# Block-sparse attention with a gated convolution network: one written-out instruction order replaced by another

## The chip, the cores and the metric

The kernel runs on one core of one Trainium2 chip. The metric is device time in microseconds (us). Three runs of the kernel before took 207.28 us in the median (207.2 to 207.51). One further execution was taken by the hardware profiler; every row of a profile below is from such an execution.

## The reference

Inputs are q, k, v of 4 batches, 8 heads, 768 tokens and 64 dims, a table of sampled blocks, and three weights (512x1024, 3x1024, 1024x512). Cut to what is computed:

```
scores = q @ k.T / sqrt(64)
mask   = band of 32-token blocks | first/last block row and column | 3 sampled key blocks per query block
attn   = softmax(where(mask, scores, -1e9));  x = heads joined of (attn @ v)     # 768 x 512 per batch
h      = relu(x @ w_in)                                                          # 768 x 1024
conv   = 3-tap convolution of h along the tokens, one weight per channel
out    = (h * sigmoid(conv)) @ w_out                                             # 768 x 512
```

## The kernel before, in words

**Pairs, segments, units.** Heads are taken in pairs; pair P = 4b + j holds heads 2j and 2j+1 of batch b, 16 pairs in all. The query tokens of a batch are cut in two segments of 384 tokens; the last of the eight is cut again into 256 and 128, so segments are numbered 0 to 8. Within a segment the program goes through its four pairs, their two heads and six key chunks, in blocks of 128 keys by 128 queries. Eight blocks are a **unit**; units are numbered 0 to 143 and are in the same order in both kernels.

**One unit.** TensorE writes the scores of a unit into one of two PSUM tiles `st` of 1024 columns (L762; the mask is 24 extra rows of both operands, with -8000 where a key block is left out). ScalarE takes the exponential of the tile into one of six tiles `pt` (L774). TensorE multiplies `pt` with the values (L799) into one of two PSUM tiles `av`, 65 columns a block, the 65th being the sum of the weights. Unit 0 is split in two halves with a tile `st` each. After the last unit of a pair, VectorE takes the reciprocal of the sums (L707) and multiplies (L709) into `xtok`.

**From attention to the network.** `xtok` is transposed into `xT`, for segments 1 to 6 by a DMA transpose that SyncE issues (L718), for segments 0, 7 and 8 by TensorE and a copy (L728). When the four pairs of a segment are there, TensorE multiplies `w_in` with `xT`, eight groups of 128 channels (L896, tile `mix`), ScalarE (L916) or VectorE (L918) takes the relu, VectorE computes the convolution (L954 multiplies, L962 adds), ScalarE the tanh that stands for the sigmoid (L1001), VectorE the gate (L1004, L1009 into `gT`). For segment 8 TensorE does the convolution (L973, L978). The `w_out` product takes 128 tokens at a time (L831), ScalarE (L327) or VectorE (L331) copies it out to `o2s`, and SyncE sends it (L840).

**Loads.** Batch 0 and half of batch 1 come in untransposed; TensorE transposes q and k (L460, L500, L522), and copies put them into the tiles `t`. Later pairs go through DMA transposes into `stg`. Most loads are issued by GpSimd (L239); tiny copies into `pace` (L407, L673) hold GpSimd back until a unit's exponential or an earlier load is there. 45 products of zeros (L230) stand at the start to keep TensorE running.

**What sets the order.** The program first makes a list of 1787 steps, each a small function that emits one or a few instructions. `put_down` reads the string `ORDER`: two characters name a step, one letter the engine where a step may go to two of them (P, A, V for TensorE, ScalarE, VectorE), one character the buffer for each tile that the step takes. The steps are emitted in just that sequence, so the order on each engine, the choice between ScalarE and VectorE and the buffer numbers all come from the string. Engines work in their own order; semaphores hold a step until its inputs are there and its buffer is free. A step that waits holds all steps behind it on its engine.

Of the kernel before, what the change touches and what calls it, by code (L numbers as in the profile page):

```python
# [25 lines left out]
6y36g2016h6B16C6D46l1RV1QV2wV36m16G06H6u1s1n6v6z5Y06I51p4X1w4Y2X14Z1x4+2Z14/2+501y511z5234222V5ZV21V6n26P16Q6R0
6A6E6F6U06V6J6K1j6o6L06M6p06W16S06Z16+6T6N16qV6OV1r6/2720732e02fV2gV743ih16X77178iiik07f07g794il1q7k17l7h51i
ijV002KV47m0in16Y707p07q7r1imViF0iGiHiI71ioipV17u17v7w2iJiq0ir7C075762z1isViK2AV42BV7D7H17I7E32C07a7b17i7j7niN1
7c17J42s17M07N2tV7o7s7t7x537R17S2DV2uV2EViO147y7O57z2iP7AiQiz1iLiR7T03007W07X7Y17diAit082183iBA2842iu870887F17G
ivV37K7L2N18938c18d7PiM07Q7U7V2OV02PViw07e1iS312/18h0ixiyV8i7Z7+0852Q17/0iV2iW8e48j58p18q3823j38r0868a8b8f8u08v  # L30
2SViT80iYiX8w18g8k8l8z18A2RV7BiC08s18B28E08FiD8G3iU8J18K8L4iEVj918R08S8tja8x8T58y8C8D8W18H8X8I36254378/090iZi+
j13jf0jg8Y09112YV0j28m18nj4j333V32Vi/941958M8N08U8V8Z8+92939c09d962j5j01mj63919h19ijh979e498jbj7j89j5ji158O29m0
9n9r19sjc818ojjA09o1jdA13ajo0jp9w09t29909a35V18P3f3g33cV3bV553i3d0562F057jl1jmjnA9x9E19FjqV3eV2jJ08Q23k09y3ju0
jv9f09g9J0jKjM9K9G0jLjwVjN9k9l9p3h3o2T13p19q9L49O19Pjr19u2G09T09U9v9z2HV2IV9Q5jO9B19Cjs9/1jx09A19V2jyjzAa0a139D
9b3r3s0jtVjR1jSjP3w1jUjA1jBa402U0jCA3l9Ha5a91aaa619I9M9NjD1jEae09Raf9Sab42VV2WVaj1jFAjZ2jTjVjQj+ag53u3tjWak9W9X
jG0a20jH9Y2k09Zj/al0jIAar0a3a7a8kv13Dacasadaw1axjXjYkj0ahat3ay1aB0aiamaCan1auavkk3E13G3Ak1k53k6k7k8k9k29+k3k4
aD4kaaG1aHao1azaAkwaI5aO0aEaFaPklkx3B23F3M3N0aQ2aT1aUaV0kbkckmknV23nVapaJkyaY0aZb11b2aK3v43xkzA33qV33zV3yVa+3
b31kE0kFkB1kCb60b7aR0aS3H0aL0be1kDV14kGAkZ0k+k/l0kK0kLbfaWb84kMAbg5kH1kIbj0kJV53I1bkkQ0l1bl2kRkSAbo1kT13P3Q23S
kAjekobpaXbt0a/bub0b4l2bq03mVaMl51l6bv3kN0kOb5kUl8kPV6ld2bB1bCb9ba1bb2bD1kVA7kW0bG0bHbhkXbI4bibmbnbL1brl73R3XbM
bcbsbwbxbQ0bRaq03T0jkaNkYAbN5bS2kd1bd3JbE0bFkebV1bWkp0lelfl9lall3c10l3lg3CV4lhkqbJbKkrl41by1lbbObPbX0c2c61lic33  # L40
3UkfkgkhA3bzlmljlolnlplcc7c813OV0bAkslqlk3LVbTbUlz1bYcb0ccbZ1c4cg1lrls3KV3VV13WVcd4ktA1b+0b/c5c9cachci5lAlBcelC
lDA2co0cpct1cfculI0lF1lGlHVlJlKVm10cjm2m4cq0cv3cy0czm3m5cD1ckcEcA4cF53+3/343403Y141kilt1lL0cr0cl2cmcI0lMlNAcscJ
lulO0lPcwcQ1cK2cR4c4d0m6lQVm91mam7mbmcm8cS1lvlwcxcV0cWcBcCcG3ZV1c+1c/cHlxA0cX3d04lR0cL42494hd30d4c01441cN1mdcO
d50lSlU1cM1lTAlVdb1dccTcUmelWVmh2mimfdg0lX0dhl+1mklYl/dd5lZVdl1cYcZdi2d1dmd2d6d7de0m0Adn1cnmjmgku4i0dq0drd80mp3
d9mrmlmqmsmx0ds3lE4e4fdv1mtdwmD1dfdx4mmmElycP45dD0dEdI1djdkdF5dodpdtdJdudymydN0dadz1dGdHdOmnmudK24q4r1dP1dA2mo
mFmzdBmvmwdS1dT46V247VdU3mAmBV34a24gd+0d/mGdLe31dMdQe4mHV1e04e52dC24jmY0e80mV1e9mWdRed1dVeemZdW4v4n4s4tea04E4F2
mXV08m+VdX1nh0njdY4w1ei0n21n3ejm/0n0ef5e10eq1ere2e6e7ebdZmI4o0ek14Jn1A94bV2ev0n50ecewes4ninkn4Anlegehex2np1el
em1eA1eBeC0en0nq4kV3eonsepn6etn7Aaeun81n9eF0eGeN1eOnaAnx2eyezeDnb0nceH5eS0eEeTeInrnt4lVeP1eJne1eX1eYeQ0eK2eL4u
4m4xnyndAbeU4eZ2nmnunznfnAmJ0mKeRngVnF3nGnB4pV3f00eVeMmLf1f51eWf6nvnnnHno0f25mP1mQmMfd0fef71mNA2ff4nCnInwnJ4yV4
mRe+e/fi1mSfjf34zVnDmTA0fn0f4o30o4fk2o5Ao61foo7fs1ftfp54G4Bo8Vot0ounEov4C14H4I4PnKnL4Q2fu3nN0nOf8f91fa1nMnT1ow  # L50
fA0fBnUfgnPfF1nVmC4K0484LoxfbfC04DA4fGfH1oyfhnQnRV1fK0nWflfLnZ0fmnXV3n+fc04RV0oz4MV04NVo01o1fP1fM4fQfU0fqfrfvfV
fwn/Ao2AfR2oAol1omfx0onfW5oofyopfD0oc0g01g1g23o91fEodg50oeAg6g70oqfInSoafJobVoB2oDoCof0ga1fNgbfOgc1fSoggf0ggoi1
fTfXfY1ojg3g4g8orohAgh4okAgn1gog9gs0gtoEfZ2osoX0oYgdmOnYfzf+oFoJ3oLgp2oKoMoGmU4A4Ogx1geoHgu5gygigjgq0oR1oSgrgv
gwf/gG0gHgk1oNoIgz3gloOgL1gMgI0gN1gAoToZgBoPoQoUo+gQ0gC0oVV1gDgRgZ1p71g+gS4g/2p8p9pah20h3h71o/V2h45pbV3gmpd0pe
pg1phpfV1cpiVh8hg0pm0pnh93poApB0pDpj1pkhhhl1gE0plAdgJ1gKgOgPhmgFA1hi0oWp0hn1pp1ps0gTgUpqh00h1h5pCpEhq0h6ptpFpG
prAehahbhrpuApJ1pKhs4gV2gWpLpMhz1hj1hc1pNhdhAgX1gYVpHpR2hkpOpv0pwhohe1hE0hFhphthuhfApxAfpy1pzpI1pSp10p2hB2hG5
pAAhv0pThwpPhC0hN1hOhP3p3hDhx1pUpQpVpWhyVhW0hHhJ2p4p5A0qk1hI1qlpZ3hKp+p/qmAghXqq0qrh/1hY0qsAhq0pXq1qB0qDq2qR1pY
q3qChQqh1hRq4qihL0i0i80i9hMA2hZ0h+q50q6i11i2q7q8qjAiia4i41hS0i5qn1i30ibqt2hTicquqSq9A1qwid2qEi60qoi7AqpAjqb0qc
ieqFhU1hVAqvqGqdif1qJ3igAqxpcqHqeqfA2ri1rjrkAqyqKqIqLqMqzr90rarbArA1qUqArf1rBrC0qNrgrhArc0rl0rmrdrn2qgqap6reAqO
qTrorprDqPqVqQrv1rwr31rq0r4rrrs2rtrurx3qWryrzrErL0rR1rF0r5rMrGrHrNrOqXqYrIrSrTrUr6rJA3rPA2rKrVVrWrQr7A1r8qZ0q+  # L60
# [997 lines left out]
```

## Time and profile before

| | before |
|---|---|
| median of three runs | 207.28 us |
| the profiled execution, first to last instruction (span) | 205.4 us |
| median less that span (the profiled execution has no other time of its own) | 1.9 us |
| TensorE products, busy | 197.1 us (96%) |
| TensorE weight loads, busy | 142.3 us (69%) |
| ScalarE, busy | 189.7 us (92%) |
| VectorE, busy | 184.9 us (90%) |
| GpSimd, busy | 59.4 us (29%) |

How to read it: busy is the union of the instructions' durations on an engine. TensorE's products overlap in its pipeline, so their busy time holds latency too, and their mean duration is longer than the distance from one to the next. ScalarE's and VectorE's durations also overlap a little with the next instruction's. The three engines are all busy for nine tenths of the span, so no single share tells which one sets the end at a given place.

### The profile page before, as it was taken

The page shows a single profiled execution, that of the slowest core. Times are in us where ns is not written, and L with a number is a line of the kernel's source. Part 1 is how long each engine was busy: PE and PEld are TensorE (multiplying, and loading weights), DVE is VectorE, ACT ScalarE, POOL GpSimd, SP SyncE. Part 2 cuts the span into 40 slices and gives each one's busy share as a digit, 9 for nine tenths or more (in the row PEclk, how much of TensorE's full clock was granted, in tenths as well). Part 3 has the DMA queues.
Part 4 walks back from the last instruction along what each step waited for, and adds up shares of the span by engine and source line. Part 5 has one row for each costly group of instructions (what it writes and reads, how often), then busy time and mean ns, then how long its engine had stood idle before and what let it go on. Part 6 is the DMA issues. An engine that isn't in the chain of part 4 may idle for free.

```text
span 205.4 us, 6237 instructions
## 1 busy us (share of the span) xinstructions
PE 197.1 (96%) x2392; PEld 142.3 (69%) x2409; DVE 184.9 (90%) x572; ACT 189.7 (92%) x253; POOL 59.4 (29%) x113
## 2 busy tenths in 40 slices
...
GB/s 155 196 190 154 186 178 114 197 127 88 154 150 126 125 103 138 218 166 163 95 105 226 97 117 123 175 154 126 14 174 88 21 123 51 3 2 3 153 3 204
DMA packets 50969, 25.59 MB, mean 125 GB/s; under 512 B 36764, under 2 KB 47996, under 8 KB 50940
## 3 DMA queue, kind: packets, MB, share of 16 engines
...
q10 hardware_dynamic: 288, 0.30, 0.5%
q14 instruction: 10, 0.08, 0.1%
HBM read 23.09 MB, written 6.29 MB: 143 GB/s over the span
## 4 chain that ended last, share of the span: by engine, by line
PE 68%; ACT 15%; DVE 12%; issue 3%; ACTq 0%; DVEq 0%
PE st L762 22%; PE mix L896 15%; PE mix L831 15%; PE av L799 12%; ACT pt L774 11%; DVE m L954 3%; DVE t L331 2%; DVE m L962 2%; ACT m L1001 1%; DVE xtok L709 1%; PE st L831 1%; ACT vt L327 1%; DVE diag L379 1%; ACT hE L916 1%; PE mix L728 1%
## 5 line engine op out<-in xcount | busy, mean ns | idle before, releaser
L774 ACT ACTIVATE pt<-st 128x1024 bf16<-128x1024 f32 (+1 forms) x145 | 142.2, 1051 | 4.2 <-PE st L762 3.7
L762 PE MATMUL st<-t 88*128 88x256 bf16 (+2 forms) x600 | 90.5, 267 | 2.3 <-DVE t L331 1.2
L799 PEld LDWEIGHTS <-pt 128*128 128x128 bf16 x1152 | 54.0, 97 | 14.2
L762 PEld LDWEIGHTS <-t 88*128 88x128 bf16 x600 | 48.9, 97 | 21.0 <-issue 1.9
L799 PE MATMUL av<-vt,pt 128*128 128x65 bf16 x1152 | 60.5, 193 | 0.1
L896 PE MATMUL mix<-xT,winb 128*128 128x384 bf16 (+2 forms) x288 | 55.2, 307 | 0.1
L954 DVE TENSOR_SCALAR m<-hE,cw 128x382 bf16<-128x382 bf16 (+2 forms) x192 | 49.1, 312 | 0.4 <-ACT hE L916 0.2
L831 PE MATMUL mix<-woutb,gT 128*128 128x512 bf16 x167 | 47.2, 379 | 0.7
L962 DVE TENSOR_TENSOR m<-m 128x764 bf16<-128x764 bf16 (+2 forms) x64 | 34.1, 532 | 0.6
L896 PEld LDWEIGHTS <-winb 128*128 128x128 bf16 x288 | 24.0, 97 | 9.2 <-issue 0.6
L1001 ACT ACTIVATE m<-m 128x764 bf16<-128x764 bf16 (+2 forms) x32 | 27.1, 853 | 0.0
L831 PEld LDWEIGHTS <-gT 128*128 128x128 bf16 x200 | 17.1, 97 | 10.0 <-DVE gT L1009 1.2
L407 POOL COPY pace<-pt 1x1 bf16<-1x1 bf16 x24 | 6.4, 268 | 54.1 <-ACT pt L774 54.0
L916 ACT ACTIVATE hE<-mix 128x384 bf16<-128x384 f32 (+2 forms) x39 | 19.8, 519 | 0.4 <-PE mix L896 0.2
L1009 DVE TENSOR_TENSOR gT<-m,hE 128x764 bf16<-128x764 bf16 (+3 forms) x36 | 18.2, 509 | 0.4
L709 DVE TENSOR_TENSOR xtok<-av,rcp 128x384 bf16<-128x384 f32 (+2 forms) x36 | 18.3, 507 | 0.4
L239 POOL DMA_DIRECT2D nat<-in_q_dram x23 | 17.3, 752 | 3.8 <-DMA nat<-in_k_dram 1.6
L918 DVE TENSOR_SCALAR hE<-mix 128x384 bf16<-128x384 f32 x25 | 13.7, 553 | 4.3 <-PE mix L896 3.7
L331 DVE COPY t<-mix 64x384 bf16<-64x384 bf16 (+1 forms) x33 | 13.2, 411 | 0.6 <-PE mix L460 0.2
L239 POOL DMA_DIRECT2D nat<-in_k_dram x15 | 12.0, 803 | 3.0 <-issue 2.4
L1004 DVE TENSOR_SCALAR m<-m 128x764 bf16<-128x764 bf16 (+3 forms) x36 | 11.9, 334 | 0.7 <-ACT m L1001 0.7
L327 ACT COPY o2s<-mix 128x512 f32<-128x512 f32 x15 | 9.2, 613 | 3.3 <-PE mix L831 3.2
...
## 6 DMA issues: line engine op xcount, KB each, us to landing
...
```

Source lines behind the costliest of these rows:

```text
L239: return op(name, {eng: occ}, lambda e: on(e).dma_start(out=dst(), in_=src), prio, deps, dma=(kind, service), **kw)
L709: nm = op("norm", {"DVE": t_dps(128 * C)}, lambda e: nc.vector.tensor_tensor(out=xtok_t[xk.index][:, 0:C].rearrange("p c h d -> p h c d"), ...
L762: nc.tensor.matmul(out=st[:, 128 * x:128 * (x + n_)], lhsT=t[0:88, 12 + 6 * hh + kc, :], rhs=t[0:88, idx:idx + (n_ - 1) * (2 if P < NPE el ...
L774: nc.scalar.activation(out=pt_t[ptb.index][:, c0:c1], in_=st_t[stb.index][:, c0:c1], func=AF.Exp, bias=0.0, scale=0.125)
L799: nc.tensor.matmul(out=o[:, off:off + 65], lhsT=pt_t[ptb.index][:, 128 * x:128 * x + 128], rhs=V_t[vslot_b[P].index][:, hh, kc, 0:65], sta ...
L831: nc.tensor.matmul(out=acc(), lhsT=gT_t[gb.index][:, ffc, 128 * t:128 * t + 128], rhs=woutb[:, ffc, c0:c1], start=(ffc == 0), stop=(ffc == ...
L896: nc.tensor.matmul(out=mix_t[hb.index][:, w1 * y:w1 * y + w1], lhsT=winb[:, fc, 128 * ffc:128 * ffc + 128], rhs=xT_t[xt_buf[n].index][:, f ...
L916: nc.scalar.activation(out=dst, in_=src, func=AF.Relu, bias=0.0, scale=0.5)
L954: nc.vector.tensor_scalar(out=m_t[cb.index][:, x, y, 0:w], in0=hE_t[heb.index][:, f0 + y, t0 + x:t0 + x + w], scalar1=cw[:, x, f0 + y:f0 + ...
L962: nc.vector.tensor_tensor(out=m[:, a_, :, 0:w], in0=m[:, a_, :, 0:w], in1=m[:, b_, :, 0:w], op=ALU.add)
L1001: th = [op("tanh", {"ACT": t_act(2 * w) + 0.04}, lambda e, cb=cb, w=w: nc.scalar.activation(out=m_t[cb.index][:, 0, :, 0:w], in_=m_t[cb.in ...
L1009: nc.vector.tensor_tensor(out=gT_t[gtb.index][:, f0:f0 + 2, t0:t1], in0=m_t[cb.index][:, 0, :, 0:w], in1=hE_t[heb.index][:, f0:f0 + 2, 1 + ...
```

## The change

Only the string `ORDER` is another (41 lines of characters become 40). The list of steps, the tiles, the transfers and the functions are the same; the new order was found by a search that judges an order by a replay with lengths read from the trace. The core of the diff:

```
 ORDER = """
-000211g010M030405060708090a0S0T1T01U230251262h12j20U0L0O0N0P0Q0R0b0c0d0e0f0g0h0i0j0k0W1e0V0X12V13A17V1AV30Y1CA
-1DA1f1d1E01K10l1H01FA00Z1LV10V0/A0m0n0o0p0q5805911JV1BV1h1GA1IA0r0s0t0u0v1M05a05b0w0x0y0z0A0B0C0D5e05f1NA0+16V
...
+0M0L0S00010211d0N0T0O031T2040W0P05060Q071U0U13A08090R0a12A0V1g0b0c0d1AA117V1O12312530e0f1CA1e1DA0Y1E11K00g0h0i
+1BA0j0Z0k1FA0261/00l0m0n0o0p0q1GA0r1LV0s0t1H00/A10V1IA1JV0+0u5802d25915a21M011A5e016V1h5f5b1j1NV18V0v0w0x0y5j11f
...
 """
```

What the two built programs show when their instructions are set side by side:

- **TensorE** has the same products. The scores stay in unit order; the other products move between them, mostly by zero to three units. The values' products follow their unit's scores after less other work. The first `w_in` product of segment 3 stands after the scores of unit 78 instead of 82. Before the first transposition stand 13 long and 1 short product of zeros instead of 13 and 6, and 14 short ones two steps later.
- **44 steps change between ScalarE and VectorE.** ScalarE issues 3 output copies (16 to 13), 3 relus (39 to 36), 2 copies of v and 2 of `xT` less; it takes over at the start 2 casts of q, 1 copy of `nblk` rows and 1 of mask rows. VectorE has the opposite.
- **GpSimd** issues the same loads, with the second half of pair 0's q five places earlier and k of pair 3 three places later among the first ones, and its paces in a slightly other sequence.
- **SyncE** has the copy of the mask rows (L343) after two of the first transposes of `xtok` instead of first; the transposes of segment 5 come in the order of pairs 0, 2, 3, 1 instead of 0, 1, 2, 3; many outputs go out in another order.

More of the change, by code (lines that the diff above doesn't have):

```diff
@@ L20 @@
 ORDER = """
-000211g010M030405060708090a0S0T1T01U230251262h12j20U0L0O0N0P0Q0R0b0c0d0e0f0g0h0i0j0k0W1e0V0X12V13A17V1AV30Y1CA
-1DA1f1d1E01K10l1H01FA00Z1LV10V0/A0m0n0o0p0q5805911JV1BV1h1GA1IA0r0s0t0u0v1M05a05b0w0x0y0z0A0B0C0D5e05f1NA0+16V
-1SA05j11V15k0E5g15c05d1Y05l211V18V191WV11XV5o05p5q35h1k15i0F1+V1ZV5t15u0G5m0H5n5C05D1O02k1/12d22x31b1a2v21l24V1
-0I0J5r5v45s4S5E55H15I2702a15M05N5J05O10K5R15S5T25w5x15F5G28V22bV2cV29V5+05/5K5L5P6035y02iV21t5z1o631642l1654680
-692o05Q6d16e5U2mV32nV2pV2qV6a55V5A16i06j6f06106266671c5W12y5BV06r16s6k11u1P06b6c4T2r34U2J04V2L04W1v2M6t26w05X6x
@@ L26 @@
[L26 to L60, printed above, removed]
@@ L61 @@
-q/r0r1A0r2
+0M0L0S00010211d0N0T0O031T2040W0P05060Q071U0U13A08090R0a12A0V1g0b0c0d1AA117V1O12312530e0f1CA1e1DA0Y1E11K00g0h0i
+1BA0j0Z0k1FA0261/00l0m0n0o0p0q1GA0r1LV0s0t1H00/A10V1IA1JV0+0u5802d25915a21M011A5e016V1h5f5b1j1NV18V0v0w0x0y5j11f
+0z195g35k1SV22h21V05l11Y15o00A1WV12j21+A0B5c05p1ZV0C1XV0X5q50D0E5t10F2x00G5d1a5u5h5i5v45m5C024V15D1b5n0H4S2k5r5s
+0I0J5E05H15I2y5J22705M028V25N4T2v11u2r35w29V2a10K5O15x15R12bV5S2cV5F5G5K5T34U1k05L5+01l5y25z5/5P6052J01c2iV45Q
+631642l04V6542L36802mV3695U5V6102o16a14W6d12M1v2nV6e1i2qV62665A06f22pV6i06j1P14X5BV1676k31w6b6r16s2wV05W05X1RV
@@ new lines @@
+2006c6t422V6w01QV6x6g21V6h6y15Y16l6B16C6m16n25ZV6u6D56v6o6G06H1o6p06I36z2e11t6A6P16Q2fV1n4Y6E2X16F6R06U06qV6J6V
+6K4Z6W51x6L06M6S06Z16+6T6/36N06OV6X720732gV1s6Yik074077178il7941r1q2KV3ih1ii7f0ijV0dimA7g4+7k12Z17h27liF2in1iGio
+707m171iH4/7p07qipVj75767a7r57b1iI7u17v2z1iJ7w07i7C0iq02AV4iriK7j7D7c02BVisV7H17E37n2s13017d2+7I2C02tV7o7s7J450
+7t2DV1y7x7M02EV7NiN02uV7e07yiz0517O21z7R17S7z1iL7F0it1iM17T07G7W07XiO2YV2iA7Y3821iP837Kiu528413417LiQ7A8707B88
+iBVb7P7Q8957U7ViR7Z7+15336214ivVf852N0iS8c12OV08d8h0iw17/08e4iT8i2PV86ix548j2808a8p18qiyV818b2Q08r38fiV38u08viW
@@ new lines @@
+8giC18w1318z1iY8A8kiD378B48E02SViU8F390552RV8l8s0iEV8t8G08x8J1iX8m28Kj908L52/1j118R03f3g18Sj28y8C3j38D8T3iZ8Hjf1
+8W1i+8n8X8I8/08Mj3j48o8N18Y132V90jai/912jg8Uj53i3a3d094133V958Vj68Z8+56j02F09c0929d1m382964933hj78O0jhjbj83k19e2
+9h11p9ijc8P9j5ji159m097jjV33bVjdA19n9r19s9o3jl0jm3cV989t0jo13eV03rjp3s03o579w0991jnVjqA9x35V19E19a9y19F2T13p19f0
+9gjJ0ju0jvjK9G2jr19J0jL3l9KjMjwA9k9l9L49pjsjN9O1jtV9q2G09PjO8Q22HV9u9T0jR19U9Q39v9zjS9A1jx19b2IVjy9V5jU9H9/1jzV
+jTa0jA09Ia103w0je9B2jBa40jV9Ma5jCA9N9RjPjW2U19C9S9W9Xa20a912WVaajG0a61jQjX2VVjHab4jZ3ae0afjYag3a3jD1j+aj13D3E33u
@@ new lines @@
+akjEj/jIAa73tal09Y0k0a8ar0asacadah3Akj03B0at4aw1axaijFVk1k52k7kv1ay53GaB0k6amaC9Zkwk2k8aG19+aHan1aD1k9auavazaAkk
+k3kak4aEaO0aPkxklaFaI0kb9D3v4kcaQ4aT1aU3xkyaV3kmkzV0aY0aJknV2aZkA3PkB13Fa+1ao23nVkCaKapkE03M3Q1kFaq1kDA1gb10kGA
+aR0b23yVaL1kH13zVaMb30b61b7aSjkaW3qV2kZ0kIaXb84aNa/be0kJV3bfb0k+b4bg5b53Sbj13N2k/bkb9ba1l0kK0bl4bo0l1kLbp3CV4bh
+bikMAbt1kN1bb03mVbq2bmbubckQ0kRbv5l52bdkSVbnbB0bCl6kObrbD3kT03OV3bG1l8kUkPA4l7bHkVAjbsbL0ld3kW1bI1kokXle3I13H0bw
+l9kYAbMbxbE0lf3T0bQ1bN4bRbFll1kd1lnbJbKbObPkp0bS0lm3JbV0lgby2l2bW3+kebz3RbX3kflobA3X3/2kqlplal3bTlhbUc11c2c60c31
@@ new lines @@
+kgc7lbl40bYlibZ1khV3krks3KVc85lI1ktV03Ulqcb1lJ3LVcc433Y2lF0ljlKAcg0lrc440chlclGci4c5c9lHVcalz1b+2lkcd5lAco0lsm12
+cplBcq1ct13VV1lCm2cucecfcv0cy0m3m4lL041b/czlMlDA2cA3lNVcD1cjckcr0cscwm5cxcElO13WVcF54clP4d3cI0lQVlt0cJm9042macQ1
+lucBm6cK2cCmbcR49lv4a0mccS0cV0cGmdcWlwcX3c+14hlU1lV4emecl1lxV1c/m7lylR0cmkucHd04cLmf3ZV0d30441lSd4d55m8lWVcM1cT
+db1cUdccN0c00lTVcYlX1dd2cZd1mh1dg0dhmilY4fdi0dl1cOd2dmmkl+0cPdn4l/lZVdq0d6drmjm0Ad7de045mgdfds1djdkmldv1dwmx1mp3
+dx34i0dD0mymq4gmrd82dEdommdI14qmsmD0cndF0mnmtmEdp4r2modtmududydJd9dN0mF4vdK4mvdadz1dO46V2dGmzmwdP2dS14n4bV2dT4j
@@ new lines @@
+dHdA1mGdLdU0dMmAmHV1dQdRmBA0d+147VmId/4sdVe304w1e04e4mV1mY0e51dWmWdX2dBe81mZmXV1he94E4F1ed0m+Vea5eee10m/14kV34o2
+e2n0nh2ef2ei14tejn1Vbn20ek34lVe6n3e7ebn4Veq0ecerniev1es5n81dYewegn9np04K0ex1eheln50nqen0nreA0eBnaAnkem1kin6eC44u
+etlEeF1eueyn7V3dC2ez4BeG4C0nseH5eD4pV34JeEeN0eO4Gnb0njnceP3eoeIeS1nx1eTepne1eU2nteX0nfndVdeJeQ0ngAeY4xeReK1eVeZ1
+f01eLf1mP1nyf25eWeMnlmJ04HnF3e+mKnuf50nGmLdZnInmf6fd1nznAmQf70femCe/nvf3mMnBff3f4mR4yV4mSnnmNA14InHfi0nCf8fjmTV3
+4Pfn14Q1fofk1no0f91o61fgnwfho30fp34zVo4o7nD4DV0fs0o5AflnJfto8AfA1nEnT04L48nKot2fmfqfrfu4ovnN1fBoumOnOfC0fa0nPow
```

10 lines of the change are left out of this document (added).

## The prediction

> **What bounds the kernel now.** I read the page first, then the chain of waits, then the busy times of stretches, then the start in order of time.
>
> ```profile
> span 205.4 us, 6237 instructions
> PE 197.1 (96%) x2392; PEld 142.3 (69%) x2409; DVE 184.9 (90%) x572; ACT 189.7 (92%) x253; POOL 59.4 (29%) x113
> PE 68%; ACT 15%; DVE 12%; issue 3%; ACTq 0%; DVEq 0%
> ```
>
> The chain that ended last is TensorE's for 68%. Its busy time holds latency, so I take its pace from stretches in which it ran without a break. Pieces of the chain of waits (start, length, what, count):
>
> ```profile
> 50.93 0.86 PE mix L831 x4
> 52.23 0.97 PE av L799 x32
> 53.21 0.88 PE st L762 x8
> 79.27 1.30 PE mix L896 x8
> 182.92 0.88 PE mix L896 x8
> 201.79 0.58 ACT o2s L327
> ```
>
> One `w_out` product of 512 columns takes 0.215 us, one values' product 0.030, the four of a unit's scores 0.44, a `w_in` product 0.163 (256 columns, in the row at 182.92: 0.11). From the code: 144 units x 0.44 = 63.4; 1152 x 0.030 = 34.6; 224 x 0.163 + 32 x 0.11 + 32 x 0.055 (128 columns, half of 256) = 41.8; 184 x 0.215 + 16 x 0.11 = 41.3. Together 181.1 us. Some 99 transposes of 128 columns add an estimated 5.3 (a quarter of 0.215 each), the convolution 1.3. From the first scores (7.01, below) to the last copy out (201.79) are 194.8 us, so TensorE lacks work or input for only 7 us of it. No order removes the products; only these 7, the start and the end can shrink.
>
> Where do they lie? The stretches (start:end, length, then busy us and instructions of PE, PEld, DVE, ACT, POOL):
>
> ```profile
> 16.00:77.00 61.00, 60.24 (x833) 45.48 (x836) 58.74 (x185) 60.60 (x73) 25.18 (x53) 1.00 1.03 142
> 77.00:124.00 47.00, 46.67 (x547) 32.42 (x552) 43.42 (x122) 46.22 (x59) 15.05 (x27) 1.00 0.98 147
> 124.00:187.00 63.00, 62.60 (x744) 45.06 (x749) 57.58 (x175) 59.70 (x83) 6.51 (x12) 1.00 0.46 84
> ```
>
> ScalarE is the one without room up to 77 us (60.60 of 61): there the exponentials set the pace and TensorE fills up behind them. After 124 it has 3.3 us free while TensorE has 0.4. So: **ScalarE first, TensorE afterwards**, with VectorE close behind both.
>
> **The change part by part.** *The start.* The rows of before, in order of time:
>
> ```profile
> 1.06 3.29 PE L230 MATMUL av<-warm 128*128 128x256 bf16 x19 [1.06 <-DVE warm L223]
> 1.67 1.28 ACT L327 ACT_TABLE_LOAD   x1 [1.67 <-PEq L1042]
> 2.97 0.70 ACT L327 COPY t<-nblk 24x384 bf16<-24x384 bf16 x1
> 3.69 1.07 ACT L327 CAST nat<-o2s 128x384 bf16<-128x384 f32 x2
> 4.22 0.53 DVE L331 CAST nat<-o2s 128x192 bf16<-128x192 f32 x1
> 4.67 0.47 ACT L327 COPY t<-mix 64x384 bf16<-64x384 bf16 x1
> 6.21 0.40 ACT L327 COPY t<-mtok 24x256 bf16<-24x256 bf16 x1 [1.08 <-DVE mtok L299]
> 7.01 0.60 PE L762 MATMUL st<-t 88*128 88x384 bf16 x4 [1.25 <-DVE t L331]
> 7.67 1.07 ACT L774 ACTIVATE pt<-st 128x512 bf16<-128x512 f32 x2
> 9.13 0.83 ACT L327 CAST vt<-m 128x768 bf16<-128x768 f32 x1
> 9.87 6.51 ACT L774 ACTIVATE pt<-st 128x1024 bf16<-128x1024 f32 x7
> ```
>
> ScalarE now copies both `nblk` halves (2.97 + 2 x 0.70 = 4.4), casts the first q (nothing shows that on ScalarE; 192 columns lie between 0.2 and VectorE's 0.53, I take 0.3, near half of one 384-column cast, 1.07/2): 4.7; two k casts: 5.8; second q cast: 6.1; two copies of 0.47: 7.0; the mask rows: 7.4. Unit 0 starts near 7.45, 0.4 late, though the 1.08 us wait in that row has been filled. Its first exponential can follow at about 7.9 (before, a copy ran until then), then a mask copy (0.40) and the second half (0.5). Unit 1's exponential comes near 9.3 instead of 9.87, since the copy of v (0.83) and one copy of q (0.47) have gone to VectorE. Another copy of q goes in after unit 2: unit 3 starts near 11.6 instead of 11.73 (9.87 + 2 x 0.93, from 6.51/7). I take **0.0**, bounds -0.4 and +0.5.
>
> *ScalarE up to unit 64.* The groups:
>
> ```profile
> L774 ACT ACTIVATE pt<-st 128x1024 bf16<-128x1024 f32 x143 | 141.1, 1057 | 4.2 <-PE st L762 3.7 <-ACT hE L916 0.3
> L916 ACT ACTIVATE hE<-mix 128x384 bf16<-128x384 f32 x31 | 15.8, 524 | 0.1
> L327 ACT COPY o2s<-mix 128x512 f32<-128x512 f32 x15 | 9.2, 613 | 3.3 <-PE mix L831 3.2
> L327 ACT COPY vt<-vn 128x768 bf16<-128x768 bf16 x1 | 0.9, 919 | 0.0
> L331 DVE COPY o2s<-mix 128x512 f32<-128x512 f32 x8 | 5.5, 690 | 2.9 <-PE mix L831 2.9
> L331 DVE COPY vt<-vn 128x768 bf16<-128x768 bf16 x14 | 5.0, 354 | 0.0
> L918 DVE TENSOR_SCALAR hE<-mix 128x384 bf16<-128x384 f32 x25 | 13.7, 553 | 4.3 <-PE mix L896 3.7
> L954 DVE TENSOR_SCALAR m<-hE,cw 128x382 bf16<-128x382 bf16 x96 | 25.1, 316 | 0.1
> L962 DVE TENSOR_TENSOR m<-m 128x764 bf16<-128x764 bf16 x32 | 17.5, 547 | 0.2
> ```
>
> Between the exponentials of units 4 and 64 ScalarE loses one output copy and one relu, 0.61 + 0.52 = 1.13; instructions overlap (an exponential lasts 1.057 but repeats every 0.93), so 0.88 of that: **-1.0**. It counts in full because ScalarE has no room there. Bounds -1.1 and 0 (TensorE might not follow).
>
> *Afterwards.* Units 64 to 100 lose three more output copies, 3 x 0.61 = 1.8. But TensorE has 0.3 us free of 47 there: faster exponentials leave it the same products. I take **-0.2**, bounds -1.6 and 0. Then two relus, two copies of `xT` and a copy of v (0.92) go, and one output copy comes; with 3.3 us of free ScalarE, nothing. The last products and the last copy out are the same: 0.
>
> *VectorE.* By the last normalisation of segment 4 it has issued, against before, 5 output copies more (3.5), one relu (0.6), 6 multiplications (1.9), one addition (0.5), one v copy (0.4), and some 1.8 less of the start's copies: +5 us. Its free time is 2.3 + 3.6 us in the first two stretches, so it just fits, provided that it hardly waits. Who waits for it is SyncE's transpose of `xtok`, and behind that the first `w_in` product of a segment, with all of TensorE. Segment 3 is the tight place:
>
> ```profile
> 89.67 0.53 PE L799 MATMUL av<-vt,pt 128*128 128x65 bf16 x12
> 92.76 0.19 DVE L707 RECIPROCAL rcp<-av 128x6 f32<-128x6 f32 x1
> 93.10 0.55 DVE L709 TENSOR_TENSOR xtok<-av,rcp 128x384 bf16<-128x384 f32 x1
> 93.78 1.21 SPq L718 DMA_TRANSPOSE xT<-xtok  x1
> 100.69 1.46 PE L896 MATMUL mix<-xT,winb 128*128 128x384 bf16 x8
> DMA to landing us min/median/max: 2.4/3.8/6.1
> ```
>
> Its last values end at 90.2 and its `w_in` starts at 100.69: 10.5 us of other products. In the new order 40 values' products, 4 units' scores and 16 `w_out` products stand between: 1.2 + 1.8 + 3.4 = 6.4. The way from values to landed `xT` is 93.78 - 92.76 = 1.0 and 3.8, or 4.8; so VectorE may be 1.6 late, and before it was 2.6 late (92.76 - 90.2). If that stays, TensorE stands 1.0; with VectorE on time, 0. I take **+0.3**, bounds 0 and 1.3.
>
> *Cost taken as nothing.* GpSimd's reordered first loads: k of pair 3 is issued some 2 us later, covered by ten units of about 1 us until it is transposed; uncovered it would be those 2 us. SyncE's outputs wait for nobody's sake; ahead of a transpose one costs it 0.4 to 0.6 of issue, within the slack above.
>
> Sum: 0.0 - 1.0 - 0.2 + 0.3 = -0.9: span 204.5, and with the 1.9 us around it, which I keep from the median, **206.4 us**.
>
> *A rule that speaks against this sum.* The Trainium skill (Perfetto Trace Analysis, Identifying the Most-Contended Engine) holds that TensorE's busy share misleads and that weight loads' busy share tells its headroom. That share is 69% in the row above, which would put ScalarE (92%) ahead all through. I trust the 181 us of counted products more; what the rule would give is rival 5.
>
> *A second rule.* The start's row at 1.06 holds 13 long products:
>
> ```profile
> L230 PE MATMUL av<-warm 128*128 128x256 bf16 x13 | 3.0, 419 | 1.1 <-DVE warm L223 1.1
> L762 PE MATMUL st<-t 88*128 88x256 bf16 x216 | 39.4, 272 | 0.4 <-ACT pt L774 0.2
> ```
>
> The same 256 columns last 419 ns at the start and 272 later, so TensorE begins slower. Now only one short product follows instead of six, then a pause of about 1.2 us before the first cast is there. The Trainium skill (TensorE: Matmul & The Clock Gate, What's actually happening) says that the clock rises after a busy window of about 3.4 us which runs free of the kernel. The two rows agree with a slow beginning; that its end varies, no run here shows.
>
> **The rivals.** Faster or slower begins at 0.2%, 0.4 us, about what a measurement of this kernel can tell from no change.
>
> 1. *ScalarE relieved early, TensorE holds later* (the forecast): 206.4, own range 205.6 to 206.8. For it: 60.60 of 61. Chance 0.38.
> 2. *TensorE's 7 us shrink further*: the forecast takes 1.2 of them, before segment 3's wait. If 2.6 go, since ScalarE's earlier exponentials leave TensorE more to choose from, 204.7. For it: 1.8 us fewer copies on ScalarE between units 64 and 100; against: 0.3 us free there. Chance 0.18.
> 3. *VectorE takes the place of the wait (slower).* At the ends of segments 3, 4, 5 and 6 `xtok` comes late and TensorE stands in front of the `w_in` product. In segment 5 a transpose of an earlier pair now stands behind that of the last pair, 1.2 more. It decides from the point where VectorE is over 1.6 us behind the values. Price: 1.0 in segment 3, 1.2 in segment 5, an estimated 0.2 in each of the others, whose distance is shortened by less; 2.6 against 1.2 of gains: **208.7**. All four at 1.2 would give 210.9. For it: +5 us in 5.9 of room; against: the page lists 4.3 and 2.9 us where VectorE waits for `mix`, waits that it can drop. Chance 0.30.
> 4. *The order does not do what it says*: gains and new waits cancel, 207.3. Chance 0.08.
> 5. *ScalarE sets the end throughout* (the first rule's case): all its steps count: 3 x 0.61 + 3 x 0.52 + 0.83 + 0.92 less 0.70 + 0.40 + 2 x 0.3 = -3.4: 203.9. Against: 3.3 us free after 124. Chance 0.03.
> 6. *TensorE stays slow until unit 3*: units 0 to 2 at twice 0.44 delay the exponentials, two of them by the whole 0.44: 206.4 + 0.9 = 207.3. Chance 0.03. The Trainium skill's second rule is its ground.
>
> **How the numbers follow.** Faster: 1, 2, 5 = 0.59. Same: 4 and 6 = 0.11. Slower: 3 = 0.30. The likeliest is 1. The range goes from 204.4 (a third of 2 and all of 5 lie below: 0.09) to 209.2 (a third of 3 lies above: 0.10).
>
> **What would show it.** Right: unit 3's exponential within 0.5 us of 11.73; ScalarE still full in 16:77, with unit 64 a us earlier; TensorE's products at the same pace; `w_in` of segment 3 near 94 to 96. Wrong: idle time of TensorE before L896 with `xT` as releaser, VectorE above 46 of 47 us in the second stretch, or a first exponential past 8.5.

## The result, and the profile after

The new order took 218.12 us in the median of six runs (216.3 to 219.4), the old one beside it 207.3 (207.2 to 208.11). The ratio is 1.0516, 95% interval 1.0479 to 1.0554: slower by 5%. The forecast was 206.4 in a range up to 209.2, so the sign was wrong, and rival 3, which had the right sign, was 9 us short. The profiled execution of the new kernel, the slowest of its six runs (219.4), spans 217.6 us against 205.4, so the traces below show 12.2 us of loss where the medians show 10.8. Each ratio leaves out runs over 1.5% above their kernel's fastest, but for new_less_mul, where all four are in it.

In the new kernel every line number is one less than before, since the string has one line less: L761 is the scores, L895 `w_in`, L717 the transposition of `xtok`. The page of the new kernel, the rows that answer to those of before:

```profile
span 217.6 us, 6163 instructions
PE 203.8 (94%) x2392; PEld 145.8 (67%) x2409; DVE 186.3 (86%) x578; ACT 191.1 (88%) x247; POOL 61.7 (28%) x113
PEclk9999999999999999999699999999999999999999
PE 40%; DVE 40%; DMA 9%; ACT 4%; issue 3%; SPq 2%; another core or an unknown queue 1%; ACTq 0%; DVEq 0%
```

Busy times have hardly changed, since the work is the same. The chain has: VectorE went from 12% to 40%, transfers from nothing to 9%, ScalarE from 15% to 4%. The same stretches as in the prediction (PE, PEld, DVE, ACT, POOL):

```profile
16.00:77.00 61.00, 59.73 (x836) 45.85 (x838) 58.23 (x182) 60.26 (x70) 28.85 (x54) 1.00 1.05 140
77.00:124.00 47.00, 44.62 (x511) 30.57 (x513) 42.08 (x118) 41.48 (x51) 13.52 (x25) 0.96 0.80 121
124.00:187.00 63.00, 59.91 (x676) 41.03 (x681) 52.30 (x156) 57.22 (x72) 9.82 (x18) 1.00 0.65 104
```

All three engines have *more* free time after 77 us than before, VectorE too. They wait for one another. Where the time went is plainest from how much later each unit's first scores begin than in the old kernel, in us, from the two traces:

| unit | 0 | 4 | 16 | 64 | 76 | 84 | 100 | 104 | 112 | 116 | end |
|---|---|---|---|---|---|---|---|---|---|---|---|
| later by | 1.9 | 3.1 | 4.0 | 4.5 | 5.1 | 8.9 | 8.9 | 9.6 | 9.4 | 12.3 | 12.2 |

There are three places. 4.0 us are lost by unit 16, 3.8 between units 76 and 84 (where segment 3's `w_in` begins), 2.9 between 112 and 116 (segment 5's). The rest of the way costs 1.5 in all. A lag at one unit also holds products that the new order has put ahead of that unit's scores, or taken from there, up to about 1 us: at the last unit, 143, it is 10.7.

**The start.** ScalarE's and TensorE's rows of the new kernel:

```profile
4.26 1.18 ACT L326 CAST nat<-o2s 128x192 bf16<-128x192 f32 x3
7.18 0.35 ACT L326 CAST nat<-o2s 128x192 bf16<-128x192 f32 x1 [1.74 <-DMA o2s<-in_q_dram]
7.44 0.97 ACT L326 COPY t<-mix 64x384 bf16<-64x384 bf16 x2
8.88 1.01 PE L761 MATMUL st<-t 88*128 88x384 bf16 x4 [0.80 <-ACT t L326]
10.29 1.03 PE L761 MATMUL st<-t 88*128 88x128 bf16 x4
13.46 0.63 PE L761 MATMUL st<-t 88*128 88x384 bf16 x2
```

The cast of q that the new order puts on ScalarE waits 1.74 us for its transfer, with the copies of k behind it. And TensorE's scores last 1.01 us for four where the old kernel's row at 7.01 has 0.60: it still runs at half speed. By the clock records of the trace full speed came at 15.66 us, in the old kernel at 3.88.

**Segment 3.** VectorE, SyncE and TensorE, in order of time:

```profile
94.34 0.38 PE L761 MATMUL st<-t 88*128 88x128 bf16 x2
94.56 0.41 PE L798 MATMUL av<-vt,pt 128*128 128x65 bf16 x8
94.96 1.92 DVE L953 TENSOR_SCALAR m<-hE,cw 128x382 bf16<-128x382 bf16 x8
97.26 0.19 DVE L706 RECIPROCAL rcp<-av 128x6 f32<-128x6 f32 x1
97.48 0.56 DVE L708 TENSOR_TENSOR xtok<-av,rcp 128x384 bf16<-128x384 f32 x1
98.45 1.22 SPq L717 DMA_TRANSPOSE xT<-xtok  x1
101.76 0.33 PE L895 MATMUL mix<-xT,winb 128*128 128x384 bf16 x1
103.90 0.32 PE L895 MATMUL mix<-xT,winb 128*128 128x384 bf16 x1 [1.81 <-DMA xT<-xtok]
```

VectorE comes to the reciprocal 2.4 us behind the last values (about 94.85), much as in the old order (92.76 - 90.2 = 2.6). The transposition lands 5.45 us after its issue, and TensorE stands 1.81 us. Then comes a second loss. Single microseconds around it; the column behind POOL's is the granted clock:

```profile
103.00:104.00 1.00, 0.10 (x1) 0.10 (x1) 0.97 (x3) 0.00 (x0) 1.00 (x2) 1.00 0.75 144
104.00:105.00 1.00, 1.00 (x7) 0.55 (x5) 0.97 (x3) 0.50 (x1) 0.86 (x2) 0.71 0.82 101
105.00:106.00 1.00, 1.00 (x9) 0.77 (x8) 0.78 (x3) 0.00 (x0) 0.00 (x0) 0.50 1.21 163
107.00:108.00 1.00, 1.00 (x10) 0.54 (x8) 1.00 (x4) 0.72 (x2) 0.00 (x0) 0.59 0.11 10
```

After the wait TensorE ran at half speed for 3.41 us (104.41 to 107.82 by the clock records), which is 1.7 us of work lost; it is the 6 in the page's clock line.

**Segment 5.** SyncE, VectorE and TensorE:

```profile
138.76 1.11 SPq L839 DMA_DIRECT2D out_dram<-o2s  x2
139.96 4.65 SPq L717 DMA_TRANSPOSE xT<-xtok  x2
147.66 0.56 DVE L708 TENSOR_TENSOR xtok<-av,rcp 128x384 bf16<-128x384 f32 x1 [2.80 <-DMA xT<-xtok]
153.41 0.68 DVE L330 COPY o2s<-mix 128x512 f32<-128x512 f32 x1
154.15 0.48 PE L895 MATMUL mix<-xT,winb 128*128 128x384 bf16 x2 [1.54 <-DVE o2s L330]
```

VectorE stands 2.80 us before a normalisation, for a tile `xtok` that an earlier transposition still reads. A copy out comes later in its queue, and TensorE stands 1.54 us before `w_in` until that copy frees the tile `mix`. The copy, number 11 of 25, is one that the change gave to VectorE.

### The profile page after: what moved, and what is told of

Read it like the earlier page. It is cut to its first block, busy times and chain, and to the rows that moved or that the text cites. A ratio compares the mean times of both kernels' runs of the same rounds, so it can differ in the third digit from the quotient of the medians.

```text
span 217.6 us, 6163 instructions
## 1 busy us (share of the span) xinstructions
PE 203.8 (94%) x2392; PEld 145.8 (67%) x2409; DVE 186.3 (86%) x578; ACT 191.1 (88%) x247; POOL 61.7 (28%) x113
## 4 chain that ended last, share of the span: by engine, by line
PE 40%; DVE 40%; DMA 9%; ACT 4%; issue 3%; SPq 2%; another core or an unknown queue 1%; ACTq 0%; DVEq 0%
PE st L761 12%; DVE m L953 11%; PE mix L895 9%; PE mix L830 8%; PE av L798 6%; DVE m L961 6%; DMA xT<-xtok 6%; DVE t L330 5%; DVE hE L917 4%; DVE xtok L708 4%; DVE gT L1008 3%; ACT pt L773 3%; DMA o2s<-in_q_dram 3%; DVE o2s L330 2%; DVE m L1003 2%
## 5 line engine op out<-in xcount | busy, mean ns | idle before, releaser
L773 ACT ACTIVATE pt<-st 128x1024 bf16<-128x1024 f32 (+1 forms) x145 | 140.6, 1019 | 8.9 <-PE st L761 7.0
L761 PE MATMUL st<-t 88*128 88x256 bf16 (+2 forms) x600 | 95.1, 273 | 2.7 <-ACT pt L773 0.9
L798 PEld LDWEIGHTS <-pt 128*128 128x128 bf16 x1152 | 55.9, 98 | 14.9 <-ACT pt L773 1.1
L761 PEld LDWEIGHTS <-t 88*128 88x128 bf16 x600 | 48.7, 98 | 24.9 <-issue 5.6
L798 PE MATMUL av<-vt,pt 128*128 128x65 bf16 x1152 | 63.0, 194 | 0.6
L895 PE MATMUL mix<-xT,winb 128*128 128x384 bf16 (+2 forms) x288 | 56.5, 310 | 4.1 <-DMA xT<-xtok 2.2
L895 PEld LDWEIGHTS <-winb 128*128 128x128 bf16 x288 | 24.2, 98 | 10.6 <-issue 3.4
L406 POOL COPY pace<-pt 1x1 bf16<-1x1 bf16 x24 | 7.7, 320 | 56.2 <-ACT pt L773 56.1
L917 DVE TENSOR_SCALAR hE<-mix 128x384 bf16<-128x384 f32 x28 | 15.3, 552 | 6.5 <-PE mix L895 6.4
L915 ACT ACTIVATE hE<-mix 128x384 bf16<-128x384 f32 (+2 forms) x36 | 17.3, 495 | 1.8 <-PE mix L895 1.7
L238 POOL DMA_DIRECT2D nat<-in_k_dram x15 | 11.6, 773 | 6.5 <-PE mix L459 4.2
L238 POOL DMA_DIRECT2D vn<-in_v_dram x15 | 10.9, 727 | 7.6 <-DVE vt L330 4.9
L330 DVE COPY t<-stg 64x1536 bf16<-64x1536 bf16 x20 | 11.2, 560 | 1.8 <-DMA stg<-nat 1.4
```

The source lines that it names most:

```text
L238: return op(name, {eng: occ}, lambda e: on(e).dma_start(out=dst(), in_=src), prio, deps, dma=(kind, service), **kw)
L330: nc.vector.tensor_copy(out=dst, in_=src)
L761: nc.tensor.matmul(out=st[:, 128 * x:128 * (x + n_)], lhsT=t[0:88, 12 + 6 * hh + kc, :], rhs=t[0:88, idx:idx + (n_ - 1) * (2 if P < NPE el ...
L773: nc.scalar.activation(out=pt_t[ptb.index][:, c0:c1], in_=st_t[stb.index][:, c0:c1], func=AF.Exp, bias=0.0, scale=0.125)
L798: nc.tensor.matmul(out=o[:, off:off + 65], lhsT=pt_t[ptb.index][:, 128 * x:128 * x + 128], rhs=V_t[vslot_b[P].index][:, hh, kc, 0:65], sta ...
L895: nc.tensor.matmul(out=mix_t[hb.index][:, w1 * y:w1 * y + w1], lhsT=winb[:, fc, 128 * ffc:128 * ffc + 128], rhs=xT_t[xt_buf[n].index][:, f ...
```

## The experiments

Kernels are named by what they start from: old or new. Steps have the names of the list: `xT n` (in one expectation `x_xb n`) is the n-th transposition of `xtok`, counted from 0, `stg n` that of a later pair's q or k, `out n` an output. In the first four expectations theory A is that the start makes the loss, theory B that what follows does; later V is that VectorE has no room (that added work delays the kernel), Q that transposes stand behind other transfers in SyncE's queue, P that `w_in` is placed too early. Lags at units below are read as in the table above.

**Start against rest.** h1_old_start: old order to the scores of unit 16, new order behind. h2_new_start: the reverse. Both only cut and join the string; buffers are dealt anew where the halves differ.

> The old order up to the scores of unit 16, the new order from there (some buffer numbers are dealt again so that the two parts fit). The new order loses 3.6 us by unit 4 and 8.4 us more later. Theory A, the start's delay is carried along and also makes VectorE late, so that most of the later loss is its echo: 207 to 210 us. Theory B, VectorE has too much to do from unit 16 on, whatever the start: 218.1 - 3.6 = 214 to 215 us. Forecast's case (no later loss): 206.5.

> The new order up to the scores of unit 16, the old order from there. Theory A: the start alone costs at least its 3.6 us and, by the echo on VectorE, more: 211 to 216 us. Theory B: the old order has room on VectorE; 3.6 us or somewhat less: 209.5 to 211 us.

h1 took 220.15 us, ratio 1.0597 (1.056 to 1.0635); h2 209.48, 1.0088 (1.006 to 1.0115). The new start alone costs 2 us, and the rest costs everything even without it: the two losses do not add up to the new order's, they overlap. A falls, and B's size for h1 was too small.

**One cast at the start.** s1_cast_back takes the second cast of q back, b1_cast_early moves it in the old order:

```
 s1:  ScalarE  cast q, cast k, cast k, [-cast q 2-], copy k ...    VectorE  ... copy k 3, [+cast q 2+]
 b1:  VectorE  ... [-cast q 2-]                                    ScalarE  cast k, [+cast q 2+], copy k ...
```

> The new order with one step moved: the second cast of q goes from ScalarE, where it stands ahead of the copies of k and waited 1.7 us for its transfer, to VectorE behind its copy of k, as in the old order. If that wait is the whole of the start's loss: unit 0's scores at about 7.3 instead of 8.9 us and unit 4's at about 12 instead of 15.1. Theory A: 207 to 212 us; theory B: 214 to 216 us. If other steps of the start cost as much, unit 4's scores stay beyond 13.5 us.

> The old order with that one step moved the other way: the second cast of q on ScalarE ahead of its copies of k. It waits for its transfer until about 7.1 us, and both copies of k, the mask copy and unit 0 stand behind it. Unit 0's scores at 8.5 to 9 us instead of 7.0; if only that is carried through, 208.8 to 209.5 us; with an echo on VectorE, 210 to 212 us.

s1 took 217.37, 1.0492 (1.046 to 1.0523), b1 207.94, 1.0037 (1.0011 to 1.0063). Unit 4's scores come at 13.2 us in s1, against 15.1. The cast is a small part of the whole loss. In b1's profiled execution the transfer had landed and the cast did not wait at all; its ten runs reach from 207.25 to 209.69, and what a late landing costs there is not shown.

**Cuts further on.** t64_new_tail: old to unit 64, new behind. m64_new_middle: new only between units 16 and 64.

> The old order up to the scores of unit 64, the new order behind them. Theory V (VectorE): its extra copies and multiplications of units 16 to 64 build up a backlog that is paid when segment 3 needs its values; with the old order up to unit 64 that backlog is missing, so the 3.8 us that TensorE stands in front of segment 3's first w_in product mostly go: about 211 us. Theory Q (SyncE's queue): the loss is made where transposes of xtok stand behind other transfers in SyncE's queue, all of them after unit 64: the new order's 7.4 us of extra standing after unit 64 (13.2 to 22.6 against 8.8 to 10.8 before) stay, 207.4 + 7.4 = 214.8 us or more.

> The old order up to the scores of unit 16, the new one from there to the scores of unit 64, the old one again behind them. Theory V: the backlog of VectorE is made here and handed over, so segment 3's w_in product waits although its place is the old one: 210 to 211 us. Theory Q: only the one us that TensorE lost between units 16 and 64 (4.1 against 3.1 of standing) remains: 208.4 us.

t64: 220.25, 1.0538 (1.0517 to 1.0559); m64: 212.63, 1.0257 (1.0234 to 1.028). Both parts cost. t64 begins unit 64 level with the old kernel and is 3.4 us late at unit 76 and 7.8 at unit 84 (with 3.41 us at half speed from 104.24 on), so the backlog of earlier units isn't needed; m64 hands over a VectorE that waits 2.82 us for a `stg` transposition at 85.48 and costs TensorE 2.25 there. Neither theory's pair of numbers came out.

**Queues and engines undone one at a time.** sp_free changes SyncE's queue alone:

```
-stg 10, stg 9, xT 11, stg 11, out 6, out 4, stg 12, xT 12, xT 14, stg 13, stg 14, xT 13, xT 15 ... xT 19, xT 17
+xT 11, stg 10, stg 9, stg 11, stg 12, xT 12, xT 14, xT 13, out 6, out 4, stg 13, xT 15, stg 14 ... xT 17, xT 19
```

eng_old gives the 32 copies out and relus that changed engine back to their old engine, pool_old gives GpSimd its old sequence, new_out_late moves only out 6 and out 4 behind xT 14.

> The new order on every engine except SyncE, whose queue is put down so that the transposes of xtok go first: the one of segment 3's last pair ahead of two transposes of k, those of segment 4 ahead of out 6 and out 4 and of two transposes of k, segment 5's third ahead of the last. Theory Q: the 2.8 us in front of segment 4 and 1 to 2 us in front of segments 3 and 5 go: 213 to 214.5 us. Theory V: xtok itself is late, since VectorE is; the queue adds little: 216.5 to 218 us.

> The new order with each of the 32 output copies and relus that changed engine back on the engine that it had before, at its new place in the order; SyncE's queue as in the new order. Theory V: VectorE is relieved of 5 copies out and about 2 relus before segment 4's end, some 4.5 us, and TensorE stands 3 to 5 us less: 213 to 215 us. Theory Q: the same queue, the same waits: 217 to 218 us.

> The new order with GpSimd's loads and paces in the old order, all else as in the new one. Theories V and Q: the late loads are a consequence, 216.5 to 219 us. If GpSimd's loads make the loss (v of a pair came late where the start was the old one): 212 to 215 us.

> The new order with SyncE's output transfers 6 and 4 put behind the second transposition of segment 4 instead of ahead of the first. Theory Q (the queue of SyncE held by an output that waits for its copy): x_xb 12 goes at about 111 instead of 120.9 us, the four transpositions no longer come in a heap, and the 2.8 us in front of segment 4 mostly go, 215 to 216.5 us. Theories P and V: the last pair's values set it, 217 to 219 us.

Three are slower than the new order: sp_free 224.22, 1.0819 (1.0784 to 1.0853); eng_old 222.33, 1.0622 (1.0581 to 1.0662); pool_old 224.03, 1.0712 (1.0657 to 1.0766). new_out_late, 221.67, 1.0592 (1.052 to 1.0663), is no faster; its interval meets the new order's. Q as stated falls, and V's number for eng_old, 213 to 215, did not come either. sp_free shows why for Q; its VectorE and TensorE, at two places:

```profile
105.25 0.55 DVE L331 COPY t<-stg 64x1536 bf16<-64x1536 bf16 x1 [4.09 <-DMA stg<-nat]
106.46 0.48 PE L896 MATMUL mix<-xT,winb 128*128 128x384 bf16 x2 [2.10 <-DVE o2s L331]
133.98 0.55 DVE L331 COPY t<-stg 64x1536 bf16<-64x1536 bf16 x1 [3.18 <-DMA stg<-nat]
135.06 1.04 PE L831 MATMUL mix<-woutb,gT 128*128 128x512 bf16 x2 [2.93 <-DVE gT L1009]
```

With xT 11 first, the `stg` transposes behind it came later, VectorE stood 4.09 us before their copy, a copy out stood behind that, and TensorE stood 2.10 us for it. At 133.98 it happened again, with a gate behind the copy; at each place 3.41 us at half speed followed or overlapped. The wait changed its name and grew. The expectations put the 2.8 us loss at segment 4; by its unit (112 to 116) it is segment 5's.

**VectorE relieved, and loaded.** In both orders the convolution's third tap is left out on VectorE but for 8 columns, so the output lacks that tap; and in the old order the third tap's multiplication is done twice, with the same output:

```
 new_less_mul, old_less_mul:  m2 = op("mul", ..., mul(2 -> 2, w=8))    a2 = op("add", ..., add(1, 2 -> 1, 2, w=8))
 old_more_mul:                -for y in range(2):    +for y in (0, 1) * (1 + x // 2):
```

> The new order, with the third tap of the convolution left out on VectorE but for 8 columns (two multiplications and one addition of each of 16 groups become nearly empty; the result lacks that tap). VectorE is relieved of about 0.9 us a group, 13 us by the end of segment 4. Theory V (VectorE has no room, so each wait that the new order puts into its queue is handed on to TensorE): with room the waits are made up again, only the start's 2 to 3.5 us stay: 208 to 211 us. Theory Q (transposes stand behind transfers in SyncE's queue and behind late copies out, whatever VectorE does): 215 us or more.

> The old order with the same tap left out. The old order's TensorE lacked little, so both theories expect little: 205.5 to 207 us. It says how much of the new order's gain from the relief is its own.

> The old order with the third tap's multiplication done twice (32 more multiplications, about 0.46 us more a group, 7 us by the end of segment 4; the result is the same). If VectorE has the 5.9 us of room that the prediction counted by the end of segment 4, 1 to 2 us are lost: 208 to 209.5 us. Theory V (the idle time there is no room, as it lies where VectorE waits for its input): 5 us or more are lost, 212 to 216 us.

old_less_mul: 207.33, 0.9987 (0.9968 to 1.0005), no gain from 15 us less on VectorE. old_more_mul: 219.06, 1.0556 (1.0525 to 1.0587), 11.6 us lost. A doubled step is two instructions, so the whole program has 64 more multiplications (the expectation's 32 are about those up to segment 4's end), which follow one another at 0.23 us each. The rows of the old order and of old_more_mul, then old_more_mul's chain and two of its waits:

```profile
L954 DVE TENSOR_SCALAR m<-hE,cw 128x382 bf16<-128x382 bf16 (+2 forms) x192 | 49.1, 312 | 0.4 <-ACT hE L916 0.2
L954 DVE TENSOR_SCALAR m<-hE,cw 128x382 bf16<-128x382 bf16 (+2 forms) x256 | 64.2, 314 | 0.4 <-ACT hE L916 0.2
DVE 54%; PE 31%; ACT 9%; issue 4%; DVEq 0%; ACTq 0%
PEld L831 <- DVE gT L1009: 7.4, 13, 1.8
PE mix L831 <- DVE gT L1009: 4.0, 9, 1.5
```

So 15.1 us more of multiplications cost 11.6, not all of it. Up to segment 4's end all of it is paid: the last reciprocal there starts at 121.3 us against 114.7, 6.6 later, with 6.6 more of VectorE's work ahead of it and the same 6.9 us of idle time. old_less_mul is the mirror: 6.8 less of work ahead of that reciprocal, the same 114.7, 6.8 more of idle time. The old order has no room on VectorE up to there; `w_out` products wait for the gates. V holds here. new_less_mul took 215.97 (212.43 to 219.55), 1.0404 (1.032 to 1.0488): relief regains some 2 us in the median and 3.9 from best run to best run, less than V expected. In its profiled execution, the best run, VectorE has 5, 8 and 14 us free in the three stretches, and the lag still grows by 2.1 at segment 3. There a copy of v, ahead of the last normalisation, waited 2.00 us until 91.31 for a load that GpSimd had issued at 84.64.

**One part of the change alone.** In the old order, five of the copies out (1, 2, 4, 5, 6) go to VectorE at their old places; old_ev2_dve does it with two of them (1 and 5):

```
-copy out 1, 2, 4, 5, 6: A
+copy out 1, 2, 4, 5, 6: V
```

> The old order with one part of the change alone: the five copies out 1, 2, 4, 5 and 6, at their old places, on VectorE instead of ScalarE (5 x 0.69 = 3.5 us more on VectorE, 5 x 0.61 less on ScalarE). The prediction's count (5.9 us of room on VectorE by the end of segment 4): 206.5 to 208 us. Theory V (no room, each us paid): 210 to 212.5 us.

> The old order with two of the five copies out (1 and 5, 1.4 us, both ahead of segment 3's values) on VectorE. No room from the first us on: 0.86 us each as with five, 208.8 to 209.4 us. A first stretch of room: 207.2 to 207.8 us.

old_ev_dve: 211.6, 1.021 (1.0178 to 1.0243). old_ev2_dve: 208.26, 1.0037 (1.0017 to 1.0057), between the two ranges expected. Five copies of 0.69 us cost 4.3, two cost 0.7. Where, in old_ev_dve (VectorE and TensorE):

```profile
93.68 0.19 DVE L707 RECIPROCAL rcp<-av 128x6 f32<-128x6 f32 x1
93.79 0.33 DVE L1004 TENSOR_SCALAR m<-m 128x764 bf16<-128x764 bf16 x1
96.45 0.69 DVE L331 COPY o2s<-mix 128x512 f32<-128x512 f32 x1 [2.34 <-PE mix L831]
97.06 0.55 DVE L709 TENSOR_TENSOR xtok<-av,rcp 128x384 bf16<-128x384 f32 x1
99.91 0.55 DVE L1009 TENSOR_TENSOR gT<-m,hE 128x764 bf16<-128x764 bf16 x1
100.51 1.34 PE L831 MATMUL mix<-woutb,gT 128*128 128x512 bf16 x4 [1.12 <-DVE gT L1009]
102.82 0.60 PE L831 MATMUL mix<-woutb,gT 128*128 128x512 bf16 x2 [0.70 <-DVE gT L1009]
104.92 1.46 PE L896 MATMUL mix<-xT,winb 128*128 128x384 bf16 x8 [0.46 <-DVE o2s L331]
```

Copy 2 stands between the reciprocal and the normalisation of segment 3's last pair, and waits 2.34 us for a `w_out` product. The normalisation and the gates wait behind it, and TensorE waits for both, 1.12, 0.70 and 0.46 us. The lag grows from 0.9 at unit 76 to 4.2 at unit 84. In the old order ScalarE makes this copy at 95.53 without a wait of its own, and TensorE does not stand there.

**The places, and all repairs together.** new_w34_late puts the `w_in` products of segments 3 and 4, with their relus and convolutions, later:

```
-w_in of segment 3 from unit 78 on (78, 79, 79, 80, ...), of segment 4 from unit 100 on
+w_in of segment 3 from unit 80 on (80, 80, 81, 82, ...), of segment 4 from unit 103 on
```

new_fix joins this with new_out_late and s1_cast_back; new_fix_less_mul leaves out the third tap as well, as above.

> The new order with the w_in products of segments 3 and 4, the relus behind them and the convolutions behind those put later, the first by some 4 units and the following by less and less; other products come ahead of them. Theory P (place: TensorE's queue reaches the product before the way from the last values to the landed transposition can be over): the 3.8 us in front of segment 3 and the 2.8 in front of segment 4 mostly go, 212 to 213.5 us. Theory V (VectorE is without room and late; the lateness only shows at the next place): 216 to 218.5 us.

> The new order with three repairs: the second cast of q on VectorE behind the copies of k, outputs 6 and 4 late as in new_out_late, w_in of segments 3 and 4 late as in new_w34_late. Theory P: the repairs add up, 1 to 2 us of the start, 4 to 6 at the two segments: 210 to 213 us. Theory V: 214.5 to 217 us.

> new_fix (second cast of q back, outputs 6 and 4 late, w_in of segments 3 and 4 late) with the third tap left out on VectorE as in new_less_mul (the result lacks that tap). If lack of room on VectorE and the early places explain the loss together, relief lets the late places hold: 208.5 to 211.5 us. If the relief alone acts and the places are indifferent: 214 to 217 us, as new_less_mul.

new_w34_late: 218.35, 1.0532 (1.0485 to 1.0579), though its profiled start lost only 0.2 us at unit 4; new_fix: 220.26, 1.062 (1.0542 to 1.0699); new_fix_less_mul: 218.76, 1.0453 (1.0382 to 1.0525). P falls for these shifts (the old order has segment 3's first at unit 82): moved back, `w_in` no longer waits, but VectorE waits for it and others wait for VectorE. new_fix lies above V's range too. new_w34_late:

```profile
103.71 0.61 PE L831 MATMUL mix<-woutb,gT 128*128 128x512 bf16 x2 [0.80 <-DVE gT L1009]
106.82 0.56 DVE L918 TENSOR_SCALAR hE<-mix 128x384 bf16<-128x384 f32 x1 [1.19 <-PE mix L896]
112.39 0.56 DVE L918 TENSOR_SCALAR hE<-mix 128x384 bf16<-128x384 f32 x1 [0.96 <-PE mix L896]
117.32 0.40 PE L799 MATMUL av<-vt,pt 128*128 128x65 bf16 x8 [1.44 <-DVE vt L331]
```

**What stays open.** VectorE's want of room and its copies out are shown in the old order. In the new one no repair that was tried gives the loss back, neither alone nor three together, and relief of VectorE leaves 8.5 us in the median, 5.4 from best run to best run. That these are the sum of many small waits, each engine's queue being fitted to the others', is the reading left over; it was not shown. No order faster than the old one was found.

## Why the prediction was wrong

**The start (0.0, bounds -0.4 and +0.5): wrong, measured +4.0 at unit 16.** The cast of q was costed by its duration, and its transfer was taken to be there. Its landing varies: in the new kernel it came at about 7.15 us, in new_w34_late and new_less_mul, with the same order up to unit 16, the cast ran at once. Of the nine kernels with this cast on ScalarE, six waited, 0.28 to 1.79 us. new_w34_late:

```profile
4.27 1.57 ACT L327 CAST nat<-o2s 128x192 bf16<-128x192 f32 x4
7.18 0.60 PE L762 MATMUL st<-t 88*128 88x384 bf16 x4 [0.36 <-ACT t L327]
8.33 0.61 PE L762 MATMUL st<-t 88*128 88x128 bf16 x4
```

Here TensorE has full speed at its first scores (0.60), and the lag is 0.2 at unit 4 and 1.3 at unit 16 (0.1 and 1.6 in new_less_mul), where the new kernel has 3.1 and 4.0. So 2.4 to 2.7 of the 4.0 us come from the landing and from the clock, and 1.3 to 1.6 from the order alone. new_fix and new_fix_less_mul have one start, with the cast on VectorE: full speed came at 4.32 us in the one, at 13.48 in the other, and at unit 16 they lag by 1.6 and 3.0. The clock alone is worth about 1.4.

**Rival 6 was the right mechanism with the wrong length.** It priced half speed until unit 3 at 0.9 and gave it 0.03. The Trainium skill (TensorE: Matmul & The Clock Gate, What's actually happening) says that the release comes after a busy window of about 3.4 us that runs free of the kernel. The traces agree with a window of that length: half-speed stretches are 3.41 us long or twice that, and the new kernel's first full-speed stretch, 88.75 us, is 26 of them. The first release varies: nine kernels with the old start had full speed first at 3.7 to 6.3 us, eleven with the new one (the new kernel among them) at 4.3 to 15.7. Two of the nine had one half-speed stretch more, at 7 us, and were 0.9 and 1.0 late at unit 4. That the new start's fewer products of zeros ahead of the first transposition are the reason is likely, and was not tried.

**ScalarE to unit 64 (-1.0): wrong.** The lag grows by 0.5 between units 16 and 64. ScalarE was full (60.26 of 61), as before, and shed its copies; but VectorE had hardly more room (58.23 of 61 busy), and the chain between 32 and 99 us is VectorE's nearly throughout. The step "ScalarE is the one without room up to 77 us" failed: two were.

**VectorE (+5 us in 5.9 us of room): the step that failed.** The extra work was sized well. The last reciprocal of segment 4 came 11.0 us later (125.7 against 114.7): 4.1 of work put ahead of it, 6.9 of more idle time. The 5.9 us ran to 124 us; between 16 us and that reciprocal the old order's VectorE idled 4.8. And the room was not room. It consists of waits for inputs that arrive when they arrive, and work added elsewhere in the queue doesn't fill them: by that reciprocal old_more_mul came 6.6 us later for 6.6 of added work, and old_ev_dve lost 4.3 in all for 3.5. This is shown in the old order. In the new one relief of VectorE regained only some 2 us of 10.8, so how much of its loss this step explains stays open. The waits for `mix`, counted in VectorE's favour against rival 3, were the harm in old_ev_dve: a copy out that waits for its product holds the normalisation behind it.

**Segment 3 (+0.3, bounds 0 and 1.3): mechanism right, sizes off.** Between the last values and `w_in` stood 6.4 us of products, as counted (94.85 to 101.22), and VectorE was 2.4 late against the 2.6 taken. The landing was 5.45 us, not the median 3.8, though the row that was quoted gave 6.1 as its longest; the wait is 1.8. The other 1.7 is the clock.

**The costs taken as nothing.** GpSimd's sequence put back (pool_old) and two outputs put later (new_out_late) made nothing faster, so no run shows a price for either of these two. SyncE's queue was not free: in segment 5 VectorE stood 2.80 us for a transposition.

**Rival 3 (208.7)** named the right engine and segments. Measured against its prices: segment 3 3.8 for 1.0, segment 5 2.9 for 1.2, segment 4 0.7 for 0.2, the start 4.0 for the 0 that it took. In segment 5 the wait ran through a copy out, not straight through the transposition. Its gains of 1.2 didn't come.

**Rival 5** stood on the Trainium skill's rule (Perfetto Trace Analysis, Identifying the Most-Contended Engine) that TensorE's headroom is judged by its share of peak arithmetic or by weight loads' busy share. The weight loads' share is 67% now and ScalarE's 88%, but ScalarE holds only 4% of the chain: no run here bears the rule out.

**"What would show it":** TensorE idle before `w_in` with `xT` as releaser came, the first exponential at 9.50 (past 8.5) came, and unit 3's exponential came at 14.99, not within 0.5 of 11.73. VectorE above 46 of 47 did not: it had 42.08. A late engine shows as less busy here, since it waits as well.
